# Two transformer layers on one core: fewer load-keeping matmuls, and a plan of the order made anew with other constants

## The chip, the cores and the metric

The kernel runs on one core of a Trainium2 chip. The metric is the device time in microseconds (us) of one execution. Engines: TensorE (PE in the profile; PEld is its weight load), VectorE (DVE), ScalarE (ACT), GpSimd (POOL), SyncE (SP), and the DMA queues.

## The reference

Attention and a feed-forward block, each twice, with the same weights in both rounds. x has 2048 rows of 448 numbers in bfloat16; 16 heads of 28; 1792 hidden features.

```python
def _A_ref(x, wqkv, wo):
    q, k, v = split_into_16_heads(x @ wqkv)
    p = softmax(q @ k.T * 28 ** -0.5)
    return heads_joined(p @ v) @ wo
def _B_ref(x, w1, b1, w2, b2):
    h = x @ w1 + b1
    r = where(h > 0, h, 0)
    return (r * r) @ w2 + b2
x = x + _A_ref(layernorm(x), ...)
x = x + _B_ref(layernorm(x), ...)
x = x + _A_ref(layernorm(x), ...)
x = x + _B_ref(layernorm(x), ...)
```

(Shortened: the splitting into heads and the einsums are written as products.)

## The kernel before

**Attention.** The 2048 queries stand in blocks of 256 (the last two of the second layer have 128), the 16 heads in four groups of four. A *unit* is one head, one block of queries and two tiles of 128 keys (four tiles, where the block has 128 queries): 512 score columns. A *score group* is three units: TensorE computes their scores with row-tiled matmuls of 32 rows (L969) into one of two score buffers in PSUM, three banks of 512 columns each. ScalarE turns them into probabilities with one exponential (L994, tile `pt<-sc`). For some groups ScalarE takes two units only (1024 columns for 1536), and the third is computed on VectorE and GpSimd by a polynomial: VectorE reads the scores (L1059), squares (L1076), GpSimd makes the power of two (L1083), VectorE multiplies (L1090). A score buffer is free for the group after the next once ScalarE, and where it has a part VectorE, have read it. The probabilities then go as the moving operand into column-tiled matmuls with V (L1153, `oT`), one *pass* for each block of queries and group of heads. Normalizing takes the sums out of `oT`: by transposes on VectorE (L1222 to L1238) near the end, elsewhere over DMAs (L1256 to L1280).

**The rest of a layer.** `chain` follows a finished block of queries: the product with wo, layernorm (L537 to L647), transposes on TensorE (L587, evicted at L599), the hidden layer with relu (L1347 on ScalarE, L1349 on VectorE) and square (L1354, L1356), the product with w2 (all of these full matmuls on L684), the sum with x (L1289), and for the first layer also the q, k and v of the second. These pieces are fitted in between the score groups; a score group stands on TensorE for each exponential.

**The order.** All of it is written out by a planner at build time. `Planner` keeps a clock for each engine, and generators (`s_stream` for scores, `e_stream` for exponentials, `p_stream` for passes, `chain`, `qkv` and others) offer operations with a duration, dependences and buffers. The planner takes the one that can start first, or by priority, advances the clock, and emits the instructions at once. So durations and latencies (`Op("PE", 0.227, ...)`, `LAT`, `PAIR`) cost nothing on the chip; they only set the order in each engine's queue. `PACE` changes constants of the planner from a given score group on, `FORCE` and `SKIP` name score groups whose third unit goes to VectorE, or doesn't, against the rule in `apart`. Queues on the chip run in the order written; waits on semaphores are put in by the framework.

**Unread matmuls.** Two kinds of matmuls only load TensorE. In `s_stream`, a score group's matmuls are issued again, once to three times (`MORE`), into the same banks with the same result, where the planner's load in a window of 3.4 us is under `HOT` and there is room. In `heat`, after a score group, one or two matmuls of 128x448 (L1407) go into a bank of the m pools that nobody reads, where the planned load over 2.8 us is under `HEAT`; their operands are `ident` and `xns[0]`, one of the buffers into which layernorm writes (`xn`):

```python
            short = HEAT - pl.load(WINDOW)
            if short <= 0 or not s_left or len(units) - at[0] < HSTOP:
                continue
            k = 1 if short < 0.14 else 2
...
                    nc.tensor.matmul(t[:, 0:D], lhsT=ident[:, :], rhs=xns[0][:, 0:D], start=True, stop=True)
```

At the start, before any input has landed, `warm_up` issues matmuls of zeros (L429).

Of the kernel before, what the change touches and what calls it, by code (L numbers as in the profile page):

```python
# [32 lines left out]
EPRIO = 2.5  # L33
ASIDE = 2.0
# [6 lines left out]
PRE = 0.5  # L41
# [8 lines left out]
L0N = 7.0  # L50
L1E = 1900
L1N = 5.6
MARGIN = 1.5
LOW = 0.85
# [11 lines left out]
SLACK = 0.5  # L66
WINDOW = 2.8
C_PRIO = 1.6
V_PRIO = 8.5
V_LATE = 4.6  # L70
V_LAST = 2.5
V_AGE = 6
V_PAST = 2
# [3 lines left out]
V_WAIT = 5  # L77
NEAR = 6
FAR = 9
KEEP = 6  # L80
LAG = 12
LEAD = 15
LAST = 690
BUSY = 0.97
TB = 2.2
TB2 = 0.9
SPAN = 15
# [2 lines left out]
AEND = 0  # L90
HOT = 0.9
MORE = 1
HEAT = 0.76
HWIN = 3.4
NEAR_U = 0
LASTP = 3.2
HOLD = 6
HOLD1 = 7
SOON = 0
# [6 lines left out]
CHUNK = 1  # L106
EV = 2.9
# [11 lines left out]
CUTS = (0, 10, 16)  # L119
CH = 4.0  # L120
QP = 8.0
FORCE = (26, 42, 46, 57, 59, 85, 86, 102, 105, 106, 107, 170, 171, 332, 335, 410, 413, 462, 466, 561, 563, 565, 567,
        576, 583, 584, 597, 598)
SKIP = (12, 13, 16, 18, 21, 22, 25, 29, 44, 47, 87, 151, 153, 154, 155, 168, 331, 333, 334, 372, 373, 375, 377, 412,
        559, 560, 562, 581, 595)
PACE = {
    0: {'ASIDE': 2.0, 'BUSY': 0.97, 'CH': 4.0, 'CHUNK': 1, 'C_PRIO': 1.6, 'EV': 2.9, 'FAR': 9, 'HOLD': 6,
         'KEEP': 6, 'L0N': 7.0, 'L1N': 5.6, 'LAG': 12, 'LASTP': 3.2, 'LEAD': 15, 'LOW': 0.85, 'MARGIN': 1.5,
         'MORE': 1, 'NEAR': 6, 'PRE': 0.5, 'QP': 8.0, 'SLACK': 0.5, 'SOON': 0, 'SPAN': 15, 'TB': 1.8, 'V_AGE':
         6, 'V_LAST': 1.8, 'V_LATE': 4.6, 'V_PRIO': 8.5, 'V_WAIT': 5},  # L130
    6: {'V_LATE': 3.5, 'C_PRIO': 2.6},
    12: {'HOLD': 4, 'KEEP': 2, 'V_LATE': 5.2},
    18: {'CHUNK': 3, 'V_LAST': 3},
    36: {'CHUNK': 2},
    54: {'QP': 5},
    60: {'V_AGE': 4},
    66: {'V_AGE': 5},
    84: {'BUSY': 0.995},
    90: {'NEAR': 8, 'BUSY': 0.97},
    96: {'NEAR': 6, 'BUSY': 0.995},  # L140
    114: {'NEAR': 8},
    150: {'LAG': 5, 'CH': 5, 'SOON': 0.5},
    156: {'MARGIN': 2.5, 'L0N': 6.0},
    162: {'TB': 2.2, 'KEEP': 5},
    174: {'KEEP': 2, 'HOLD': 5, 'LAG': 8},
    192: {'MORE': 2},
    198: {'MORE': 1, 'FAR': 12},
    204: {'NEAR': 6, 'EV': 1.5, 'PRE': -0.3},
    210: {'NEAR': 8, 'EV': 2.9, 'PRE': 0.5},
    216: {'KEEP': 3, 'V_WAIT': 3.5},  # L150
    240: {'LAG': 16, 'LASTP': 2.6, 'SPAN': 11},
    246: {'LAG': 8, 'LASTP': 3.2, 'SPAN': 15, 'MORE': 2, 'V_WAIT': 2.5},
    252: {'V_LATE': 4.0},
    282: {'MORE': 1},
    288: {'MORE': 2},
    306: {'CHUNK': 3},
    318: {'CHUNK': 2},
    360: {'ASIDE': 1.0, 'HOLD': 4},
    366: {'V_AGE': 3, 'L1N': 5.8},
    402: {'L1N': 5.0, 'CHUNK': 1, 'HOLD': 6},  # L160
    414: {'L1N': 5.8},
    426: {'HOLD': 5, 'SPAN': 20},
    432: {'LOW': 0.9},
    444: {'V_PRIO': 2.8},
    450: {'V_PRIO': 8.5},
    522: {'HOLD': 6, 'V_LATE': 4.6},
    528: {'HOLD': 5, 'V_LATE': 4.0},
    534: {'PRE': 0.8, 'L0N': 7.8, 'LOW': 0.95},
    540: {'ASIDE': 0.3, 'SPAN': 11},
    552: {'LAG': 5},  # L170
    576: {'FAR': 17},
    582: {'FAR': 12},
    588: {'FAR': 17, 'V_LAST': 3.5, 'SLACK': 0.2},
    594: {'V_LAST': 3, 'SLACK': 0.5},
    648: {'KEEP': 2, 'CHUNK': 2, 'LEAD': 12},
}


class Res:


    def __init__(self, n):
        self.n = n
        self.rel = []
# [4 lines left out]


class Op:
    __slots__ = ("eng", "dur", "fn", "deps", "acq", "rel", "mode", "sets", "start", "end", "res", "turn", "ready", "lat", "need", "got", "more", "room", "port", "durs")

    def __init__(self, eng, dur, fn, deps=(), acq=None, rel=None, mode="full", sets=(), lat=0.0, need=1, port=False):
        self.eng = eng if isinstance(eng, tuple) else (eng,)
        self.durs = dur if isinstance(dur, tuple) else (dur,) * len(self.eng)
        self.dur, self.fn, self.deps, self.mode, self.lat = self.durs[0], fn, deps, mode, lat
        self.rel = rel if isinstance(rel, list) else ([] if rel is None else [rel])
        self.acq = acq if isinstance(acq, tuple) or callable(acq) else (() if acq is None else (acq,))
        self.sets = sets if isinstance(sets, list) else ([sets] if sets else [])  # L200
        self.start = self.end = self.res = self.turn = None
        self.need, self.got, self.more, self.port = need, [], 0.0, port


LAT = {"PE": 0.25, "ACT": 0.28, "DVE": 0.07, "POOL": 0.10, "DMA": 2.0, "-": 0.0}
PAIR = {("PE", "ACT"): 0.275, ("PE", "DVE"): 0.197, ("DVE", "ACT"): 0.1, ("DVE", "POOL"): 0.1, ("DVE", "DVE"): 0.035,
        ("POOL", "DVE"): 0.035, ("PE", "PE"): 0.0, ("ACT", "ACT"): 0.0, ("POOL", "POOL"): 0.0}


class Planner:  # L210
# [20 lines left out]
        self.streams.sort(key=lambda s: s[0](0.0) if callable(s[0]) else s[0])  # L231

    def earliest(self, o):
        t = 0.0
        for d in o.deps:
            if not isinstance(d, Op):
                d = self.tok.get(d)
            if d is None or d.end is None:
                return None, None
            t = max(t, d.end + d.lat + PAIR.get((d.eng[0], o.eng[0]), LAT[d.eng[0]]))  # L240
        acq = o.acq() if callable(o.acq) else o.acq
        if o.acq:
            free = [r.when() for r in acq if r.when() is not None]
            if not free:
                return None, None
            t = max(t, min(free))
        o.ready = t
        best = None
        for e, dur in zip(o.eng, o.durs):
            s = max(t, self.clock[e])  # L250
            if e == "PE" and self.mode != o.mode:
                s = max(t, self.clock[e] + 0.1)
            if o.port:
                s = max(s, self.port["POOL"] - 0.14 if e == "DVE" else self.port["DVE"] + (0.01 if self.port["DVE"] > t else 0.0))
            late = s + (dur + ASIDE * (e == "DVE") if "POOL" in o.eng else 0.0)
            if best is None or late < best[2] - 0.05:
                best = (s, e, late)
        return best[:2]

    def run(self):  # L260
        while self.streams:
# [9 lines left out]
            if due is None:  # L271
                due = next((c[0] + c[3][2].dur + LAT["ACT"] for c in cands if c[1] == 1), None)
            if due is not None:
# [23 lines left out]
            for a in o.rel:  # L297
                a.got.append(o.end + o.lat + LAT[e])
                if len(a.got) == a.need:
# [9 lines left out]
def kernel(  # L309
# [44 lines left out]
    R_sc, R_m, R_pt = Res(2), (Res(1), Res(1)), Res(NPT)  # L354
# [24 lines left out]
    more = [const.tile([P, QR], DT.float32, name=f"more{g}") for a in AHEAD[3:] for g in a]  # L379
# [439 lines left out]
    for pi, (l, qb, g, kbs, first, last) in enumerate(passes):  # L819
        r = 4 // blocks[l][qb][1]  # L820
# [6 lines left out]
    gbuf = []  # L827
# [29 lines left out]
    def apart(i, now, us, soon=SOON):  # L857
# [20 lines left out]
        if any(pl.tok.get(d) is None or pl.tok[d].end + LAT["DVE"] > now for d in needs(units[j])):  # L878
            return None
        if len(gbuf) - 1 in FORCE:  # L880
            return j
        if len(gbuf) - 1 in SKIP or pl.load(SPAN, "DVE") > (LOW if behind(i) else BUSY):
            return None
# [19 lines left out]
    def s_stream():  # L903
        while at[0] < len(units):
            gi = len(gbuf)
# [5 lines left out]
            def fn(e, gi=gi, us=us, js=js):  # L911
# [50 lines left out]
                for i in list(range(4)) * (again + 1):  # L962
                    for k, (pi, kb, r, hh) in enumerate(us):
                        if i >= r:
# [5 lines left out]
                                         lhsT=K_sb[l][rows, g, (kb + i) * P:(kb + i + 1) * P],  # L970
                                         rhs=Q_sb[rows, g, t0 * P:(t0 + nt) * P],
                                         start=True, stop=True, tile_position=(DHP * hh, 0))
            o = gbuf[gi]["s"] = Op("PE", 0.227, fn,
                                   deps=list({d for u in us for d in needs(u)}), acq=R_sc, mode="row", sets=("s", gi))
            yield o
        s_left.clear()
# [8 lines left out]
    def e_stream():  # L985
        gi = 0
        while gi < len(gbuf) or s_left:
            yield Op("-", 0.0, None, deps=[("s", gi)])
            n = gbuf[gi]["n"] * 512

            def fn(e, gi=gi, n=n):
                e_now[:] = [e_now[0] + n // 512 + ("x" in gbuf[gi]), gi]
                pt = gbuf[gi]["pt"] = ptp.tile([P, 3 * 512], DT.bfloat16, name="pt")
                t = nc.scalar.activation(out=pt[:, 0:n], in_=gbuf[gi]["sc"][:, 0:n], func=AF.Exp,  # L994
                                         scale=float(np.log(2.0)) * 2.0 ** -FRAC)
                if gbuf[gi].get("x") is gbuf[gi]["s"]:
                    apart_from(gi, t)
            o = gbuf[gi]["e"] = Op("ACT", n / 1200 + 0.051, fn, deps=[("s", gi)], acq=R_pt, need=n // 512 + gbuf[gi].get("in", 0),
                                   rel=gbuf[gi]["s"], sets=("e", gi))
            yield o  # L1000
            gi += 1
# [390 lines left out]
    def heat():  # L1392


        for gi in itertools.count(HFROM):
            if not s_left:
                return
            yield Op("-", 0.0, None, deps=[("s", gi)])
            short = HEAT - pl.load(WINDOW)
            if short <= 0 or not s_left or len(units) - at[0] < HSTOP:  # L1400
# [57 lines left out]
```

## Time and profile before

| | us |
|---|---|
| median of 3 runs | 845.28 (845.02 to 845.38) |
| the profiled execution | 845.39 |
| its span, first to last instruction | 843.3 |
| first exponential starts (from the span's start) | 10.78 |
| last exponential ends | 828.78 |

| line, engine | what | count |
|---|---|---|
| L969 PE | score matmuls, repeats among them | 5120 |
| L1153 PE | probabilities with V | 4352 |
| L1407 PE | unread matmuls of `heat` | 133 |
| L994 ACT | exponentials, 1536 / 1024 columns | 445 / 238 |
| L1059 DVE | units taken from ScalarE | 237 |

In the lines of groups, a row gives line, engine, operation, tiles and shapes, count, then busy time in us, mean ns of one, and the engine's idle time before them with what ended it. In the timeline a row gives start in us, duration in us, engine, line, operation, tiles, shapes and count; idle time before it, and its releaser, stand in brackets. In the table by stretches a row gives the stretch, its length, busy us (and count) of PE, PEld, DVE, ACT and POOL, the granted clock of TensorE, the DMA share and GB/s.

### The profile page before, as it was taken

What the parts mean: (1) busy time and instruction counts of PE and PEld (TensorE: products, weight loads), DVE (VectorE), ACT (ScalarE), POOL (GpSimd) and SP (SyncE); (2) the same over time, 40 slices, a digit from 0 to 9 for tenths busy, and PEclk for the clock granted to TensorE, in tenths of its full rate; (3) what the DMA queues carried; (4) which work ended last, traced back from release to release, by engine and by line L of the source; (5) the groups of instructions that cost most, each with busy time, mean ns of one, the idle gap of its engine ahead of it and who ended that gap; (6) DMA issues with size and microseconds to landing.
All of it is one profiled execution on the core that took longest, in us unless ns stands there. A gap on an engine that the chain in (4) does not pass through costs nothing.

```text
span 843.3 us, 28075 instructions
## 1 busy us (share of the span) xinstructions
PE 805.7 (96%) x12089; PEld 422.3 (50%) x12089; DVE 788.5 (93%) x1531; ACT 827.2 (98%) x698; POOL 210.3 (25%) x332
## 2 busy tenths in 40 slices
PE   8999999999999999999999999999999999999997
PEld 4455544454544545455445444434455454545665
DVE  7999999999999999999999999999999998989954
ACT  8999999999999999999999999999999999999994
POOL 3211322322222223322222223322212223121200
PEclk9999999999999999999999999999999999999999
DMA  9200100000000000000000000011100001000000
GB/s 244 74 3 2 26 22 12 15 15 16 8 9 16 15 15 16 15 3 15 2 3 2 2 2 3 15 29 29 32 9 14 26 15 31 21 13 15 14 20 13
DMA packets 32312, 17.94 MB, mean 21 GB/s; under 512 B 17786, under 2 KB 31739, under 8 KB 32188
## 3 DMA queue, kind: packets, MB, share of 16 engines
q1 hardware_dynamic: 32188, 16.16, 7.0%
q8 instruction: 94, 1.54, 0.8%
q14 instruction: 30, 0.25, 0.1%
HBM read 13.87 MB, written 2.06 MB: 19 GB/s over the span
## 4 chain that ended last, share of the span: by engine, by line
ACT 43%; PE 33%; DVE 15%; issue 8%; POOL 1%; DMA 0%; ACTq 0%; DVEq 0%; POOLq 0%
ACT pt L994 43%; PE mt L684 13%; PE sc L969 11%; PE oT L1153 6%; DVE r L1349 2%; DVE v_i L1059 2%; DVE v_e L1076 1%; DVE pt L1090 1%; PE mt L1407 1%; PE sc L684 1%; PE tp L587 1%; DVE K_sb L1076 1%; DVE st L537 1%; DVE x_sb L1289 1%; DVE K_sb L1059 1%
## 5 line engine op out<-in xcount | busy, mean ns | idle before, releaser
L994 ACT ACTIVATE pt<-sc 128x1536 bf16<-128x1536 f32 (+1 forms) x683 | 816.9, 1464 | 1.7 <-PE sc L969 1.4
L969 PE MATMUL sc<-Q_sb,K_sb 32*128 32x256 bf16 (+1 forms) x5120 | 301.0, 265 | 27.7 <-ACT pt L994 20.7
L969 PEld LDWEIGHTS <-K_sb 32*128 32x128 bf16 x5120 | 128.6, 92 | 209.1 <-issue 160.7
L1083 POOL TENSOR_SCALAR v_i<-v_i 128x512 int32<-128x512 int16 x126 | 89.2, 708 | 291.8 <-DVE v_e L1076 290.2
L1153 PE MATMUL oT<-pt,V_sb 128*32 128x256 bf16 (+1 forms) x4098 | 157.0, 268 | 0.8 <-ACT pt L994 0.5
L684 PE MATMUL mt<-xnT,w 128*128 128x256 bf16 (+1 forms) x928 | 121.9, 269 | 0.6 <-DVE r L1349 0.3
L1153 PEld LDWEIGHTS <-V_sb 128*32 128x32 bf16 x4352 | 89.3, 96 | 52.9 <-issue 49.6
L684 PEld LDWEIGHTS <-w 128*128 128x128 bf16 x952 | 77.6, 98 | 36.4 <-issue 28.6
L1059 DVE TENSOR_SCALAR v_i<-sc 128x512 int32<-128x512 f32 x126 | 85.7, 682 | 5.2 <-PE sc L969 4.5
L1076 DVE SCALAR_TENSOR_TENSOR v_e<-v_i 128x512 f32<-128x512 uint16 x126 | 87.6, 699 | 0.3
L1083 POOL TENSOR_SCALAR K_sb<-K_sb 128x512 int32<-128x512 int16 x64 | 45.3, 708 | 138.6 <-DVE K_sb L1076 134.5
L1349 DVE TENSOR_SCALAR r<-mt 128x512 bf16<-128x512 f32 x108 | 73.7, 682 | 5.4 <-PE mt L684 4.7
L684 PE MATMUL mt<-w,V_sb 128*128 128x448 bf16 (+1 forms) x274 | 68.3, 352 | 0.0
L1083 POOL TENSOR_SCALAR V_sb<-V_sb 128x512 int32<-128x512 int16 x47 | 34.3, 729 | 101.6 <-DVE V_sb L1076 100.7
L1059 DVE TENSOR_SCALAR K_sb<-sc 128x512 int32<-128x512 f32 x64 | 43.7, 683 | 1.9 <-PE sc L969 1.6
L1289 DVE TENSOR_TENSOR x_sb<-x_sb,mt 128x448 bf16<-128x448 bf16 (+1 forms) x61 | 37.0, 607 | 8.9 <-PE mt L684 8.5
L1407 PE MATMUL mt<-xn,ident 128*128 128x448 bf16 x133 | 44.2, 355 | 1.1 <-DVE x_sb L1289 0.3
L1076 DVE SCALAR_TENSOR_TENSOR K_sb<-K_sb 128x512 f32<-128x512 uint16 x64 | 44.1, 694 | 0.1
L1090 DVE SCALAR_TENSOR_TENSOR pt<-v_e,v_i 128x512 bf16<-128x512 f32 x59 | 40.0, 679 | 3.8 <-POOL v_i L1083 3.8
L537 DVE BATCH_NORM_STATS2 st<-x_sb 128x6 f32<-128x448 bf16 x62 | 37.7, 611 | 0.8 <-DMA x_sb<-in_A_x_dram 0.6
L684 PEld LDWEIGHTS <-V_sb 128*128 128x128 bf16 x302 | 24.1, 98 | 25.1 <-issue 12.6
L1059 DVE TENSOR_SCALAR V_sb<-sc 128x512 int32<-128x512 f32 x47 | 31.9, 681 | 1.2 <-PE sc L969 1.0
(115 smaller groups left out, 828.0 us busy)
## 6 DMA issues: line engine op xcount, KB each, us to landing
rec<-scr SPq DMA_DIRECT2D x54, 128.0 KB
x_sb<-in_A_x_dram SPq DMA_DIRECT2D x8, 224.0 KB
out_dram<-x_sb SPq DMA_DIRECT2D x15, 112.0 KB
w<-in_B_w_dram SPq DMA_DIRECT2D x1, 1568.0 KB
w<-in_B_w_dram SPq DMA_DIRECT2D x1, 1344.0 KB
dn<-oT_sb SPq DMA_DIRECT2D x54, 4.0 KB
V_sb<-in_A_wqkv_dram SPq DMA_DIRECT2D x4, 168.0 KB
scr<-dn SPq DMA_DIRECT2D x27, 8.0 KB
```

What stands on the lines that cost most here:

```text
L537: nc.vector.bn_stats(out=box["st"][:, :], in_=x_sb[:, t0 + j, :] if src is None else src())
L684: nc.tensor.matmul(box["t"][:, c0:c0 + n], lhsT=lhsT() if callable(lhsT) else lhsT, rhs=rhs, start=a, stop=b)
L969: nc.tensor.matmul(dst[k][:, i * nt * P:(i + 1) * nt * P], lhsT=K_sb[l][rows, g, (kb + i) * P:(kb + i + 1) * P], rhs=Q_sb[rows, g, t0 * P: ...
L994: t = nc.scalar.activation(out=pt[:, 0:n], in_=gbuf[gi]["sc"][:, 0:n], func=AF.Exp, scale=float(np.log(2.0)) * 2.0 ** -FRAC)
L1059: t = nc.vector.tensor_scalar(out=box["i"], in0=two(src), scalar1=EXP_BIAS, scalar2=EXP_LOW, op0=ALU.add, op1=ALU.max)
L1076: nc.vector.scalar_tensor_tensor(out=box["h"], in0=box["f"], scalar=lin, in1=box["f"], op0=ALU.add, op1=ALU.mult)
L1083: (nc.vector if e == "DVE" else nc.gpsimd).tensor_scalar(out=box["e"], in0=box["n"], scalar1=2.0 ** 22, scalar2=EXP_BASE, op0=ALU.mult, op ...
L1090: nc.vector.scalar_tensor_tensor(out=box["two"](pd), in0=box["h"], scalar=low, in1=box["e"].bitcast(DT.float32), op0=ALU.add, op1=ALU.mult)
L1153: nc.tensor.matmul(box["t"][DHP * hh:DHP * hh + DHP, 0:n], lhsT=V_sb[l][:, kb + i, 4 * g + hh, :], rhs=p[:, c0:c0 + n], start=begin and kb ...
L1289: nc.vector.tensor_tensor(out=x_sb[:, tb, lo:hi], in0=x_sb[:, tb, lo:hi], in1=t[:, 0:hi - lo], op=ALU.add)
L1349: nc.vector.tensor_scalar(out=r[:, 0:w], in0=t[:, 0:w], scalar1=0.0, scalar2=None, op0=ALU.max)
L1407: nc.tensor.matmul(t[:, 0:D], lhsT=ident[:, :], rhs=xns[0][:, 0:D], start=True, stop=True)
```

## The change

`HEAT` goes from 0.76 to 0.5. `FORCE`, `SKIP` and `PACE` are replaced by other lists (`PACE` now steps by 8 score groups, and sets `EPRIO` and `V_PAST` too, and no longer `LAG`, `NEAR`, `FAR`, `ASIDE`, `QP`, `V_LATE`, `V_PRIO` and `V_WAIT`). Some of the planner's durations and latencies get other values. `earliest` keeps the time at which an operation's dependences are met in a new field `known`, and doesn't work it out again. The engine code (which operations, tiles and buffers there are) is the same.

```diff
-HEAT = 0.76
+HEAT = 0.5
...
-FORCE = (26, 42, 46, 57, 59, 85, 86, 102, 105, 106, 107, 170, 171, 332, 335, 410, 413, 462, 466, 561, 563, 565, 567,
-        576, 583, 584, 597, 598)
...
+FORCE = (63, 65, 67, 69, 70, 72, 74, 76, 77, 78, 128, 132, 134, 144, 148, 149, 151, 162, 181, 190, 200, 201, 205, 207,
+        244, 245, 392, 396, 409, 413, 456, 548, 550, 641, 644, 645, 647)
...
 PACE = {
...
-    6: {'V_LATE': 3.5, 'C_PRIO': 2.6},
-    12: {'HOLD': 4, 'KEEP': 2, 'V_LATE': 5.2},
...
+    24: {'EPRIO': 8, 'L0N': 7.4},
+    40: {'HOLD': 5},
...
-LAT = {"PE": 0.25, "ACT": 0.28, "DVE": 0.07, "POOL": 0.10, "DMA": 2.0, "-": 0.0}
-PAIR = {("PE", "ACT"): 0.275, ("PE", "DVE"): 0.197, ("DVE", "ACT"): 0.1, ("DVE", "POOL"): 0.1, ("DVE", "DVE"): 0.035,
+LAT = {"PE": 0.25, "ACT": 0.3, "DVE": 0.07, "POOL": 0.10, "DMA": 2.0, "-": 0.0}
+PAIR = {("PE", "ACT"): 0.275, ("PE", "DVE"): 0.2, ("DVE", "ACT"): 0.1, ("DVE", "POOL"): 0.15, ("DVE", "DVE"): 0.035,
...
     def earliest(self, o):
-        t = 0.0
-        for d in o.deps:
...
+        t = o.known
+        if t is None:
+            t = 0.0
+            for d in o.deps:
...
+            o.known = t
...
-            o = gbuf[gi]["s"] = Op("PE", 0.227, fn,
+            o = gbuf[gi]["s"] = Op("PE", 0.234, fn,
...
-            o = gbuf[gi]["e"] = Op("ACT", n / 1200 + 0.051, fn, deps=[("s", gi)], acq=R_pt, need=n // 512 + gbuf[gi].get("in", 0),
+            o = gbuf[gi]["e"] = Op("ACT", n / 1200 + 0.0555, fn, deps=[("s", gi)], acq=R_pt, need=n // 512 + gbuf[gi].get("in", 0),
```

More of the change, by code (lines that the diff above doesn't have):

```diff
@@ L121 @@
 QP = 8.0
-FORCE = (26, 42, 46, 57, 59, 85, 86, 102, 105, 106, 107, 170, 171, 332, 335, 410, 413, 462, 466, 561, 563, 565, 567,
-        576, 583, 584, 597, 598)
-SKIP = (12, 13, 16, 18, 21, 22, 25, 29, 44, 47, 87, 151, 153, 154, 155, 168, 331, 333, 334, 372, 373, 375, 377, 412,
-        559, 560, 562, 581, 595)
-PACE = {
[L127 to L130, printed above, removed]
-    6: {'V_LATE': 3.5, 'C_PRIO': 2.6},
-    12: {'HOLD': 4, 'KEEP': 2, 'V_LATE': 5.2},
[L133 to L175, printed above, removed]
@@ new lines @@
+FORCE = (63, 65, 67, 69, 70, 72, 74, 76, 77, 78, 128, 132, 134, 144, 148, 149, 151, 162, 181, 190, 200, 201, 205, 207,
+        244, 245, 392, 396, 409, 413, 456, 548, 550, 641, 644, 645, 647)
+SKIP = (66, 73, 80, 81, 83, 84, 87, 135, 150, 164, 165, 178, 180, 183, 184, 188, 243, 246, 247, 281, 283, 285, 286,
+        312, 313, 317, 318, 319, 379, 381, 382, 408, 410, 412, 415, 544, 545, 549, 551, 553, 554, 643, 653, 654, 656,
+        657, 658, 659, 661)
+PACE = {
+    0: {'BUSY': 0.97, 'CH': 4.0, 'CHUNK': 2, 'C_PRIO': 1.6, 'EPRIO': 2.5, 'EV': 2.9, 'HOLD': 6, 'KEEP': 6,
+         'L0N': 7.0, 'L1N': 5.6, 'LASTP': 3.2, 'LEAD': 15, 'LOW': 0.85, 'MARGIN': 1.5, 'MORE': 1, 'PRE': 0.5,
+         'SLACK': 0.5, 'SOON': 0, 'SPAN': 15, 'TB': 2.2, 'V_AGE': 6, 'V_LAST': 2.5, 'V_PAST': 2},
+    24: {'EPRIO': 8, 'L0N': 7.4},
+    40: {'HOLD': 5},
+    48: {'SOON': 1.0, 'MARGIN': 4.5},
+    56: {'TB': 1.8, 'LOW': 0.9},
+    72: {'SPAN': 8, 'L1N': 5.0, 'TB': 3.6},
+    80: {'SPAN': 15, 'L1N': 5.6, 'TB': 1.8},
+    112: {'V_LAST': 3.5},
+    128: {'MARGIN': -1},
+    160: {'MARGIN': 4.5},
+    168: {'MARGIN': -1, 'CH': 5, 'PRE': 0.8, 'HOLD': 3},
+    176: {'LEAD': 12},
+    184: {'LEAD': 15},
+    200: {'V_AGE': 5, 'L1N': 5.8, 'V_LAST': 1.8},
+    208: {'V_AGE': 6, 'L1N': 5.6, 'V_LAST': 3.5},
+    216: {'BUSY': 1.01},
+    232: {'KEEP': 3},
+    240: {'EPRIO': 1.5},
+    256: {'MORE': 3, 'HOLD': 5},
+    272: {'TB': 2.2},
+    280: {'EPRIO': 8, 'LASTP': 2.6},
+    312: {'V_PAST': 5, 'EV': 2.2},
+    344: {'EV': 3.3},
+    352: {'MARGIN': 0.5},
+    384: {'C_PRIO': 3.2},
+    392: {'MARGIN': 4.5, 'CHUNK': 1},
+    400: {'L0N': 7.8, 'KEEP': 4},
+    408: {'CH': 3.3},
+    456: {'KEEP': 2},
+    640: {'HOLD': 3},
+    648: {'HOLD': 5},
+    656: {'SLACK': 0.2},
@@ L191 @@
 class Op:
-    __slots__ = ("eng", "dur", "fn", "deps", "acq", "rel", "mode", "sets", "start", "end", "res", "turn", "ready", "lat", "need", "got", "more", "room", "port", "durs")
+    __slots__ = ("eng", "dur", "fn", "deps", "acq", "rel", "mode", "sets", "start", "end", "res", "turn", "ready", "lat", "need", "got", "more", "room", "port", "durs", "known")
     def __init__(self, eng, dur, fn, deps=(), acq=None, rel=None, mode="full", sets=(), lat=0.0, need=1, port=False):
@@ L200, in __init__ @@
         self.sets = sets if isinstance(sets, list) else ([sets] if sets else [])
-        self.start = self.end = self.res = self.turn = None
+        self.start = self.end = self.res = self.turn = self.known = None
         self.need, self.got, self.more, self.port = need, [], 0.0, port
-LAT = {"PE": 0.25, "ACT": 0.28, "DVE": 0.07, "POOL": 0.10, "DMA": 2.0, "-": 0.0}
-PAIR = {("PE", "ACT"): 0.275, ("PE", "DVE"): 0.197, ("DVE", "ACT"): 0.1, ("DVE", "POOL"): 0.1, ("DVE", "DVE"): 0.035,
+LAT = {"PE": 0.25, "ACT": 0.3, "DVE": 0.07, "POOL": 0.10, "DMA": 2.0, "-": 0.0}
+PAIR = {("PE", "ACT"): 0.275, ("PE", "DVE"): 0.2, ("DVE", "ACT"): 0.1, ("DVE", "POOL"): 0.15, ("DVE", "DVE"): 0.035,
         ("POOL", "DVE"): 0.035, ("PE", "PE"): 0.0, ("ACT", "ACT"): 0.0, ("POOL", "POOL"): 0.0}
@@ L233, in earliest @@
     def earliest(self, o):
-        t = 0.0
-        for d in o.deps:
[L236 to L240, printed above, removed]
+        t = o.known
+        if t is None:
+            t = 0.0
+            for d in o.deps:
+                if not isinstance(d, Op):
+                    d = self.tok.get(d)
+                if d is None or d.end is None:
+                    return None, None
+                t = max(t, d.end + d.lat + PAIR.get((d.eng[0], o.eng[0]), LAT[d.eng[0]]))
+            o.known = t
         acq = o.acq() if callable(o.acq) else o.acq
         if o.acq:
-            free = [r.when() for r in acq if r.when() is not None]
+            free = [w for w in (r.when() for r in acq) if w is not None]
             if not free:
```

## The prediction

> **What bounds the kernel now.** I read the busy shares first, then ScalarE's groups by form, then the starts of single exponentials, and last the places where one starts late.
>
> ```profile
> span 843.3 us, 28075 instructions
> PE 805.7 (96%) x12089; PEld 422.3 (50%) x12089; DVE 788.5 (93%) x1531; ACT 827.2 (98%) x698; POOL 210.3 (25%) x332
> PEclk9999999999999999999999999999999999999999
> ```
> Three engines look full; the shares alone don't decide. ScalarE's groups, by form:
>
> ```profile
> L994 ACT ACTIVATE pt<-sc 128x1536 bf16<-128x1536 f32 x445 | 649.5, 1611 | 1.7 <-PE sc L969 1.4
> L994 ACT ACTIVATE pt<-sc 128x1024 bf16<-128x1024 f32 x238 | 270.2, 1190 | 0.0
> ```
> The durations overlap (445 x 1611 ns is more than 649.5 us), so what counts is the distance from start to start. Neighbours without a wait, and the last one:
>
> ```profile
> 26.45 1.47 ACT L994 ACTIVATE pt<-sc 128x1536 bf16<-128x1536 f32 x1
> 27.78 1.49 ACT L994 ACTIVATE pt<-sc 128x1536 bf16<-128x1536 f32 x1
> ...
> 30.44 1.08 ACT L994 ACTIVATE pt<-sc 128x1024 bf16<-128x1024 f32 x1
> 31.35 1.10 ACT L994 ACTIVATE pt<-sc 128x1024 bf16<-128x1024 f32 x1
> ...
> 827.45 1.34 ACT L994 ACTIVATE pt<-sc 128x1024 bf16<-128x1024 f32 x1
> ```
> A large one takes 1.330 us, a small one 0.903 (unrounded starts). The first starts at 10.78, the last ends at 828.78: a stream of 818.00 us. Its work is 445 x 1.330 + 237 x 0.903 + 1.34 = 807.2 us. So the span is 10.8 (opening) + 807.2 (exponentials) + 10.8 (late starts) + 14.5 (after the last). ScalarE sets the end, and only the three small terms, or fewer exponentials, can give anything.
>
> I went through the starts of all 683. Of the 10.8 us, 7.6 are in 54 exponentials over 40 ns late; the rest is jitter. By what stands on TensorE just ahead of the late score matmuls: 1.4 us in the opening (three, before 45 us), 2.2 in 16 behind an unread matmul of L1407, 0.8 in five whose scores are computed twice or more, 3.2 in 30 behind useful matmuls. One of the 16:
>
> ```profile
> 441.66 0.38 PE L684 MATMUL mt<-xnT,wq 128*128 128x256 bf16 x2
> 442.24 0.35 PE L1407 MATMUL mt<-xn,ident 128*128 128x448 bf16 x1 [0.19 <-DVE xn L647]
> 442.52 0.39 PE L969 MATMUL sc<-Q_sb,K_sb 32*128 32x256 bf16 x6
> ```
> The unread matmul reads xn, which VectorE was just writing; in TensorE's queue the score waits behind it, starts 0.28 us after it, and its exponential (443.02) is 0.23 us late.
>
> **The change, part by part.** It alters the planner's constants and lists, so I took the order of instructions from both built programs and priced it by rows of before.
>
> Exponentials: 444 large and 239 small in place of 445 and 238: 0.903 - 1.330 = -0.43 us on the path. The part goes to VectorE instead: 238 chains in place of 237, three VectorE operations that stand 0.60 apart, +1.8 us. VectorE is busy 775 of the stream's 818 us; that idle time covers it; without the cover it costs 1.8.
>
> Unread matmuls of L1407: 133 become 4. At 0.189 us each (four of 128x448 on L684 start 0.189 apart) TensorE gets 24.4 us back. Repeated scores, also unread, go the other way: L969 has 5300 matmuls for 5120, 30 more repeats of six. A repeat costs 0.21 us (12 take 0.61, 6 take 0.40): +6.4 us. Switches between row-tiled, column-tiled and full matmuls fall from 1404 to 1324; a switch adds 0.095 us (0.285 from a 448-column matmul to a score, 0.189 to its like): -7.6. Together -25.6 us of TensorE's issue time, some 769 before. None of it is on the path by itself: the stream of exponentials covers it. What reaches the path is lateness:
> - Behind L1407: 2.2 us, of which 0.30 (at 136.97) was held by VectorE's read of the old scores and stays. The others are late by at most 0.23, less than the 0.28 that an unread matmul puts ahead of the score. I take -1.9 (bounds -2.2 and 0, if another wait stands right behind).
> - Repeats: 170 sets make 0.8 us late; 30 more, at the same rate, +0.14 (bounds 0 and 30 x 0.21 = 6.3, if all came too late; nearest the measured rate).
> - The 3.2 us behind useful matmuls: the emptier queue should take some of it, a new order deals new ones. I take -0.9; bounds -3.2 (all gone) and +3.2 (twice as many).
> - Opening: the order is the same up to the 12 scores at 22.01. In after, four more matmuls of wq (4 x 0.109) stand ahead of them, waiting for a bank that K's eviction at 21.27 frees: +0.45 (bounds 0 and 0.5).
> - End: 14 full matmuls stand between the last wo matmul and the four transposes, in place of 13: +0.2 (bounds 0 and 0.5; below nothing is out, the chain behind is the same).
>
> The planner's durations (score 0.234 for 0.227, exponential +0.0045, three waits) emit nothing; they act through the order counted here. SP's queue has the same 184 issues, POOL one more power operation of 0.71 us at 25% load.
>
> Sum: -0.43 - 1.9 - 0.9 + 0.14 + 0.45 + 0.2 = -2.4 us. The profiled execution took 845.39 (2.1 around its span); the median shown is 845.28, 0.1 less. 845.39 - 2.4 - 0.1 = 842.9; I say 842.8.
>
> [...] L1407 keeps TensorE loaded, and the floor falls from 0.76 to 0.5. Counting only the time in which the array gets columns, the least loaded 3.4 us before the last exponentials end have 0.47, at full clock:
>
> ```profile
> 824.50:827.90 3.40, 2.36 (x67) 1.77 (x56) 1.50 (x5) 3.40 (x4) 0.00 (x0) 1.00 0.02 5
> ```
> (2.36 is PE busy, with ends that overlap; 1.00 the granted clock.) By the order of after, three score groups in a row (about 3.6 us) fall to 0.30 of ScalarE's time near group 454, and to 0.36, 0.39 and 0.42 at three other places; before, never under 0.46. So after goes where this trace shows nothing. [...]
>
> **The rivals.**
> - *VectorE holds the scores (slower).* Place: a score must wait until VectorE has read the third part of the scores two groups back (L1059); an exponential late by 0.30 us at 136.97 is that. It decides once VectorE is some 0.9 us behind. For it: VectorE has 95% of ScalarE's time filled, and the stretches between two such reads that hold more VectorE work than exponentials rise from 91 to 100. Against: summed along the order, the backlog over 0.9 us falls from 0.8 us to 0.4. If 20 of the 100 paid 0.30: 842.8 + 6 = 848.8.
> - *The clock drops (slower).* For it: the loads above. Against: 0.47 did nothing. The first matmuls, from 1.25 on, stand 0.37 apart for 0.189, and full speed is there by 7.7: some 6.5 us at half clock. 74% (median load) of that, 4.8 us, less 0.8 of spare time (12%) and 0.7 that the queue may lag, is 3.3 a place: 846.1 with one, 849.4 with two, 856 with four.
> - *The relief is hidden (same).* The scores behind L1407 were waiting for VectorE or a bank anyhow; L1407 filled the wait. For it: it is issued only where the planner saw room. Then -1.9 and -0.9 fall out: -0.43 + 0.14 + 0.45 + 0.2 = +0.4, 845.6.
> - *It doesn't do what it says.* TensorE has 51 more matmuls in all; but cheaper ones, by the count above. That changes no time of its own.
>
> **How the numbers follow.** 0.2% is 1.7 us, about what a measurement of this kernel tells from no change: faster is below 843.6, slower above 847.0. Forecast 0.54 (839 to 843.6), hidden relief 0.18 (843.6 to 847), VectorE 0.20 (847 to 850), clock 0.08 (846 to 856, mostly slower). So faster 0.54, same 0.18, slower 0.28. The likeliest one's own range is 839 to 843.6. If all lateness behind L1407 and behind useful matmuls went, with no repeat, opening or end cost, it is 845.3 - 0.4 - 2.2 - 3.2 = 839.5, and some jitter may go with it: low 838.6. High 848.8, the price of VectorE's case; beyond it lie the upper parts of two rivals, together with what is below the low some 0.17.
>
> **What would show it.** Right: L994 x444 and x239, the stream near 815.8 us with late starts of 8.8 us in place of 10.8; L1407 x4; few late scores behind L1407; first stall at 22 us up from 0.88 to some 1.3; clock 1.00 throughout; end near 14.7. Wrong: late starts of 11 us or more, the late scores ended by DVE L1059 (VectorE), or a clock row below 9 near 430 or 560 us (clock). An end over 15.5, or an opening that loses more than 1 us, would break the sum where I took it as nearly fixed.

## The result, and the profile after

The changed kernel takes 847.85 us (median of 11 runs, 845.23 to 849.88), the kernel before 845.32 (11 runs, 845.02 to 846.76): a ratio of 1.0023, 95% interval 1.0015 to 1.0032. It is slower, by 0.23%, where 842.8 was forecast. Its lines are numbered 11 lower than those of before (L983 is the old L994, L958 the old L969, L1396 the old L1407). The page's first lines and the clock row, in tenths, one digit for each fortieth of the span:

```profile
span 845.7 us, 28161 instructions
PE 787.9 (93%) x12140; PEld 424.3 (50%) x12140; DVE 787.5 (93%) x1533; ACT 827.8 (98%) x699; POOL 215.0 (25%) x333
...
PEclk9999999999999999999999999899999999999999
```

TensorE is less busy, ScalarE is as before, and one digit of the clock is an 8, at 529 to 550 us. ScalarE's exponentials by form:

```profile
L983 ACT ACTIVATE pt<-sc 128x1536 bf16<-128x1536 f32 x444 | 652.7, 1631 | 2.8 <-PE sc L958 2.6
L983 ACT ACTIVATE pt<-sc 128x1024 bf16<-128x1024 f32 x239 | 275.7, 1202 | 1.4 <-PE sc L958 1.4
```

The counts are those of the built program; idle time before them is 4.2 us for 1.7. By stretches of 3.41 us (PE, PEld, DVE, ACT and POOL busy, then the granted clock):

```profile
537.61:541.03 3.42, 2.39 (x50) 1.29 (x52) 3.42 (x8) 3.42 (x4) 0.84 (x2) 1.00 0.00 0
541.03:544.44 3.41, 3.39 (x47) 1.95 (x46) 2.38 (x5) 3.17 (x3) 1.42 (x2) 0.50 0.06 7
544.44:547.85 3.41, 3.41 (x57) 1.69 (x51) 1.97 (x4) 2.39 (x3) 0.62 (x1) 0.50 0.26 79
547.85:551.27 3.42, 2.65 (x54) 1.56 (x47) 2.98 (x7) 3.42 (x4) 1.54 (x2) 1.00 0.04 5
551.27:554.68 3.41, 2.52 (x62) 1.68 (x62) 3.29 (x7) 3.41 (x4) 0.62 (x1) 1.00 0.07 13
554.68:558.09 3.41, 2.40 (x47) 1.53 (x44) 3.34 (x6) 3.41 (x4) 0.62 (x1) 1.00 0.23 68
558.09:561.51 3.42, 3.42 (x47) 0.99 (x39) 2.76 (x6) 2.71 (x3) 0.62 (x1) 0.50 0.02 5
```

The clock is at one half from 541.03 to 547.85 and from 558.09 to 561.51. Scores then take twice as long (repeated sets of six matmuls start 0.43 us apart at 546 us, and 0.22 at full clock), and ScalarE waits, as its timeline shows (idle time in brackets):

```profile
540.57 1.65 ACT L983 ACTIVATE pt<-sc 128x1536 bf16<-128x1536 f32 x1
542.38 4.09 ACT L983 ACTIVATE pt<-sc 128x1024 bf16<-128x1024 f32 x3 [0.16 <-PE sc L958]
547.40 1.02 ACT L983 ACTIVATE pt<-sc 128x1024 bf16<-128x1024 f32 x1 [0.93 <-PE sc L958]
```

The exponentials in and just behind the two stretches are late by 3.3 us in sum. Worked out from the starts of all 683, as in the prediction, the span moved so:

| term, us | before | after | difference |
|---|---|---|---|
| first exponential starts | 10.78 | 10.48 | -0.29 |
| one exponential less of 1.330, one more of 0.903 | | | -0.43 |
| late starts, 0 to 45 us | 1.47 | 1.26 | -0.21 |
| late starts, 45 to 520 us | 5.90 | 6.20 | +0.30 |
| late starts, 520 to 590 us | 0.82 | 3.90 | +3.08 |
| late starts, from 590 us | 2.62 | 2.33 | -0.29 |
| last exponential's start to the end | 15.86 | 16.07 | +0.21 |
| span | 843.3 | 845.7 | +2.4 |

All the loss is in the stretch with the half clock. The runs say the same: at a mean clock of 1.000 the changed kernel took 845.23 (one run), at 0.998 846.36 to 846.58 (four), at 0.996 848.08, at 0.994 847.85 to 849.44 (four), at 0.992 849.88. One window of 3.41 us at half clock lowers the mean by 0.002, so a window costs about 1.2 us. And even the undisturbed run gains nothing on before: two things have to be explained.

### The profile page after: what moved, and what is told of

The parts are those of the page before. It is cut to its first block, busy times and chain, and to the rows that moved or that the text cites. A ratio compares the mean times of both kernels' runs of the same rounds, so it can differ in the third digit from the quotient of the medians.

```text
span 845.7 us, 28161 instructions
## 1 busy us (share of the span) xinstructions
PE 787.9 (93%) x12140; PEld 424.3 (50%) x12140; DVE 787.5 (93%) x1533; ACT 827.8 (98%) x699; POOL 215.0 (25%) x333
## 4 chain that ended last, share of the span: by engine, by line
ACT 46%; PE 29%; DVE 15%; issue 8%; DMA 0%; POOL 0%; SPq 0%; ACTq 0%; DVEq 0%; POOLq 0%
ACT pt L983 46%; PE mt L673 12%; PE sc L958 11%; PE oT L1142 5%; DVE v_i L1048 2%; DVE v_e L1065 1%; DVE pt L1079 1%; DVE r L1338 1%; PE sc L673 1%; DVE x_sb L1278 1%; DVE K_sb L1048 1%; DVE K_sb L1065 1%; DVE st L526 1%; DVE V_sb L1048 1%; DVE V_sb L1065 1%
## 5 line engine op out<-in xcount | busy, mean ns | idle before, releaser
L983 ACT ACTIVATE pt<-sc 128x1536 bf16<-128x1536 f32 (+1 forms) x683 | 817.0, 1481 | 4.2 <-PE sc L958 4.0
L958 PE MATMUL sc<-Q_sb,K_sb 32*128 32x256 bf16 (+1 forms) x5300 | 311.4, 267 | 47.6 <-ACT pt L983 41.5
L958 PEld LDWEIGHTS <-K_sb 32*128 32x128 bf16 x5300 | 140.8, 92 | 220.6 <-issue 172.6
L673 PE MATMUL mt<-xnT,w 128*128 128x256 bf16 (+1 forms) x912 | 119.7, 270 | 1.0 <-DVE oT_sb L1168 0.5
L1072 POOL TENSOR_SCALAR K_sb<-K_sb 128x512 int32<-128x512 int16 x66 | 47.2, 715 | 146.9 <-DVE K_sb L1065 145.7
L1338 DVE TENSOR_SCALAR r<-mt 128x512 bf16<-128x512 f32 (+1 forms) x109 | 74.0, 680 | 4.4 <-PE mt L673 3.9
L673 PE MATMUL mt<-w,V_sb 128*128 128x448 bf16 x274 | 68.5, 355 | 0.0
L1072 POOL TENSOR_SCALAR V_sb<-V_sb 128x512 int32<-128x512 int16 x45 | 32.6, 724 | 103.2 <-DVE V_sb L1065 99.7
L1278 DVE TENSOR_TENSOR x_sb<-x_sb,mt 128x448 bf16<-128x448 bf16 x61 | 37.3, 611 | 9.1 <-PE mt L673 8.8
L553 POOL TENSOR_TENSOR ve<-mv,eps_t 128x2 f32<-128x2 f32 (+1 forms) x34 | 12.5, 368 | 106.4 <-DVE mv L531 105.8
L673 PEld LDWEIGHTS <-V_sb 128*128 128x128 bf16 x302 | 24.9, 97 | 25.4 <-issue 11.4
L1079 DVE SCALAR_TENSOR_TENSOR pt<-v_e,v_i 128x512 bf16<-128x512 f32 x51 | 35.0, 692 | 1.9 <-POOL v_i L1072 1.8
```

The source lines that it names most:

```text
L553: nc.gpsimd.tensor_tensor(out=ve[:, a:b], in0=mv[0][:, a:b, 1], in1=eps_t[:, a:b], op=ALU.add)
L673: nc.tensor.matmul(box["t"][:, c0:c0 + n], lhsT=lhsT() if callable(lhsT) else lhsT, rhs=rhs, start=a, stop=b)
L958: nc.tensor.matmul(dst[k][:, i * nt * P:(i + 1) * nt * P], lhsT=K_sb[l][rows, g, (kb + i) * P:(kb + i + 1) * P], rhs=Q_sb[rows, g, t0 * P: ...
L1072: (nc.vector if e == "DVE" else nc.gpsimd).tensor_scalar(out=box["e"], in0=box["n"], scalar1=2.0 ** 22, scalar2=EXP_BASE, op0=ALU.mult, op ...
L1079: nc.vector.scalar_tensor_tensor(out=box["two"](pd), in0=box["h"], scalar=low, in1=box["e"].bitcast(DT.float32), op0=ALU.add, op1=ALU.mult)
L1278: nc.vector.tensor_tensor(out=x_sb[:, tb, lo:hi], in0=x_sb[:, tb, lo:hi], in1=t[:, 0:hi - lo], op=ALU.add)
```

## The experiments

The theories: A, the clock halves after a window of some 3.4 us with little work in the array, weighted by the rows and columns that a matmul uses; B, it follows TensorE's busy time; C, chance. For the missing gain: the unread matmuls of L1407 caused the lateness behind them (as predicted), or they only filled a wait.

**e1, a full matmul in 40 score groups.** In the loop of `s_stream`, ahead of the scores, into the score bank:

```diff
+                if 432 <= gi < 472:
+                    nc.tensor.matmul(dst[0][:, 0:D], lhsT=ident[:, :], rhs=w2[:, 0, 0:D], start=True, stop=True)
                 for i in list(range(4)) * (again + 1):
```

> The changed kernel with one unread matmul of 128x448, full array, ahead of the scores of each of the score groups 432 to 471 (about 530 to 580 us); the order of all else is the same. Theory A (the clock halves when the work in the array, weighted by the rows and columns that a matmul uses, is low over a window of some 3.4 us: 0.38 and 0.32 in the two windows before the drops at 541 and 558 us, never under 0.40 elsewhere): the pad adds some 0.14, so the clock stays at 1.00 there in every run, and the median falls from 847.9 to 845 to 846. Theory B (the clock follows the time in which TensorE is busy, whatever the shape): the same here, so this run alone does not tell A from B; its twin with a narrow matmul does. Theory C (the drop is chance, or comes from elsewhere): drops stay, the median stays near 847.9.

850.87 us (850.65 to 851.21, 4 runs), ratio 1.0063 [1.0047, 1.008]. No half clock between 500 and 600 us in the profile; the runs are at 0.998 to 1.000. The drop is gone in this trace, and of the ten runs of e1 and e2 none is under 0.998, where six of eleven of the changed kernel are; so C falls. But the median went up and not down: 40 pads put ahead of the scores make late starts of their own (15.0 us in sum, none at half clock). The miss is in what a pad costs.

**e2, the same on 32 rows.**

```diff
+                if 432 <= gi < 472:
+                    nc.tensor.matmul(dst[0][:, 0:D], lhsT=ident[DHP * us[0][3]:DHP * us[0][3] + DHP, :],
+                                     rhs=w2[DHP * us[0][3]:DHP * us[0][3] + DHP, 0, 0:D], start=True, stop=True,
+                                     tile_position=(DHP * us[0][3], 0))
```

> As e1, but the unread matmul uses 32 of the 128 rows, with the same 448 columns and about the same time. Theory A: it adds only a quarter of the work, some 0.04, so the windows before 541 and 558 us stay near 0.36 to 0.42 and the clock still drops in most runs; median 846.5 to 849. Theory B: as good as the full one, clock 1.00 and 845 to 846.

847.70 us (847.33 to 849.34, 6 runs), 1.0029 [1.0018, 1.0041]; five runs at 1.000, one at 0.998. Theory A expected drops, and there were none. In the profiled run the weighted load of the padded windows came to 0.42 at the least, above where anything dropped elsewhere (0.38 at the most), so the pair does not tell A from B.

**e3, before without L1407.** Planned as before, the time in the plan kept, no matmul issued:

```diff
             def junk(e):
-                t = bank(o, "mt")
-                for _ in range(k):
-                    nc.tensor.matmul(t[:, 0:D], lhsT=ident[:, :], rhs=xns[0][:, 0:D], start=True, stop=True)
+                pass
```

> The kernel before, planned as it was, but without the 133 unread matmuls of L1407; all else in the same order. Prediction's reason (late exponentials behind L1407 vanish): outside of stretches at half clock the late starts fall by about 1.9 us, from 10.8 to some 8.9. Rival (they waited for something else): late starts stay at 10.5 or more. Theory A: without them the weighted load falls to 0.18 to 0.30 in windows near 544 to 568 us, so the clock drops there and the median is 2 us or more above before, 847 to 853. Theory B: plain busy time falls less; few drops, 843 to 846.

848.69 us (847.23 to 850.09, 5 runs), 1.0039 [1.0025, 1.0052], clock 0.984 to 0.990. In the profiled run it halves at 546.4, 556.7 and 566.9 us. Outside of 520 to 590 us the late starts are 1.47 + 5.78 + 2.49 = 9.74 us; before had 1.47 + 5.90 + 2.62 = 9.99. So taking L1407 away gave 0.25 us there. Exponential by exponential: the 16 that the prediction puts behind L1407 were late by 2.21 us in sum, and are late by 1.39 without it. That sum hides two kinds. Eleven of the 16 now come on time (0.07 us left of 1.13), the prediction's own example among them: its score no longer waits for xn, and the exponential that was 0.23 late at 443.02 is on time, the next one (0.26 in before) too:

```profile
441.91 0.27 PE L684 MATMUL mt<-xnT,wq 128*128 128x256 bf16 x1
442.12 0.39 PE L969 MATMUL sc<-Q_sb,K_sb 32*128 32x256 bf16 x6
```

The other five are late without L1407 as well (1.08 us with it, 1.32 without). And exponentials elsewhere became later: outside of 520 to 590 us all gains add up to 1.97 us, all losses to 1.72. One place shows how. In before, a score at 158.17 stands behind L1407 at 157.88, and its exponential is 0.13 late. In e3 the unread matmul is gone, but a bias row, L684, waits for VectorE's eviction, and the score comes at 158.35:

```profile
156.95 0.40 PE L969 MATMUL sc<-Q_sb,K_sb 32*128 32x256 bf16 x6
157.50 0.35 PE L684 MATMUL mt<-b2w,one 128*128 128x448 bf16 x1 [0.16 <-DVE oT_sb L1179]
157.69 0.73 PE L684 MATMUL mt<-w,K_sb 128*128 128x448 bf16 x3
158.35 0.39 PE L969 MATMUL sc<-Q_sb,K_sb 32*128 32x256 bf16 x6
```

The exponential is now 0.38 late. VectorE is behind here since GpSimd's rstd came later, first in before, then in e3:

```profile
153.18 0.70 DVE L647 TENSOR_SCALAR xn<-x_sb,mv,rstd 128x448 bf16<-128x448 bf16 x2 [0.58 <-POOL rstd L565]
153.56 0.70 DVE L647 TENSOR_SCALAR xn<-x_sb,mv,rstd 128x448 bf16<-128x448 bf16 x2 [0.85 <-POOL rstd L565]
```

With the filler gone, another wait decided. The other losses were not followed up like this.

**e4, before with L1407 on 32 rows.** Count, order, bank and columns as before:

```diff
-                    nc.tensor.matmul(t[:, 0:D], lhsT=ident[:, :], rhs=xns[0][:, 0:D], start=True, stop=True)
+                    nc.tensor.matmul(t[:, 0:D], lhsT=ident[0:DHP, :], rhs=xns[0][0:DHP, 0:D], start=True, stop=True,
+                                     tile_position=(0, 0))
```

> The kernel before with its 133 unread matmuls on 32 of the 128 rows: the same count, order, bank, operand tile and about the same time. Theory A: as good as none for the clock, drops near 545 to 568 us, 847 us or more. Theory B: clock 1.00, 845 to 846.

850.77 us (849.77 to 854.33, 4 runs), 1.007 [1.0047, 1.0093], all at 0.986 to 0.990. The stretches of e4 around its drop:

```profile
557.88:561.29 3.41, 3.08 (x40) 1.37 (x42) 3.41 (x8) 3.41 (x4) 0.62 (x1) 1.00 0.04 2
561.29:564.71 3.42, 2.84 (x44) 1.21 (x44) 3.38 (x9) 3.42 (x4) 0.62 (x1) 1.00 0.28 84
564.71:585.19 20.48, 20.25 (x184) 8.15 (x179) 16.14 (x29) 16.38 (x14) 5.05 (x7) 0.50 0.08 20
```

and of before at the same place:

```profile
560.00:563.40 3.40, 2.90 (x43) 1.07 (x36) 3.40 (x8) 3.40 (x5) 0.62 (x1) 1.00 0.16 47
563.40:566.80 3.40, 3.15 (x41) 1.25 (x44) 3.37 (x8) 3.40 (x4) 1.60 (x3) 1.00 0.14 38
```

TensorE is busy 2.84 of 3.42 us, as in before, and the clock halves for 20.5 us; the changed kernel kept it behind 2.52 of 3.41 (551.27). Busy time doesn't decide. Theory B falls; what differs in e4 is how many rows the filler uses (and with that its tile of the array).

**e5, eight pads.** As e1, for `gi in (442, 445, 449, 451, 455, 456, 462, 466)`.

> The changed kernel with one unread full matmul of 128x448 ahead of the scores of only eight score groups (442, 445, 449, 451, 455, 456, 462, 466), those with over 0.65 us of free TensorE time; all else in the same order. Theory A (the clock halves after a window of some 3.4 us in which the work weighted by rows and columns is under some 0.35 to 0.38): the two low windows rise by some 0.06 to 0.11 each, to 0.42 to 0.45; no drop between 500 and 600 us, 1.00 in the middle. Then this run tells what the new order is worth by itself: 842.8 to 843.6 if the prediction's relief is there and only the clock hid it; 845.0 to 845.8 if the new order has as many late starts as the old one (10.4 us in the changed kernel's profile outside of the drops). If drops are not tied to the load: median 847 to 848 as the changed kernel.

845.94 us (845.54 to 847.54, 11 runs), 1.0008 [0.9999, 1.0016]. Eight runs at 1.000 took 845.54 to 846.14; three at 0.998, 847.30 to 847.54. With the clock held, the new order is no faster than the old one: the late starts are 11.4 us, for 10.8 in before (1.3 of them belong to what e6 takes out).

**e6, e5 without repeats where two units share rows.** In a score group whose three units include two of the same head of the group of four, their matmuls use the same 32 rows. In the changed kernel's timeline:

```profile
482.58 0.40 PE L958 MATMUL sc<-Q_sb,K_sb 32*128 32x256 bf16 x6
482.91 0.55 PE L673 MATMUL mt<-wv,xnT 128*128 128x448 bf16 x2
483.50 1.47 PE L958 MATMUL sc<-Q_sb,K_sb 32*128 32x256 bf16 x18
```

18 matmuls take 1.47 us, where others of 18 take 0.83 (at 539.59): those start in threes, six times 0.109 us apart; these start by ones and twos, twelve times 0.109 apart.

```diff
-                for i in list(range(4)) * (again + 1):
+                for i in list(range(4)) * (again + 1 if len({u[3] for u in us}) == len(us) else 1):
```

> As e5, and the scores are not repeated in the three groups (of 683) in which two of the three units have the same 32 rows of the array; repeats elsewhere stay, the order stays. In the changed kernel's profile a set of six takes 0.44 us in such a group and not 0.21, and three exponentials behind them are late by 0.55, 0.52 and 0.25. If the repeats there are the cause: 0.8 to 1.3 us below e5. If something else holds these exponentials: within 0.3 of e5.

845.00 us (844.54 to 849.53, 12 runs), 1.0 [0.9989, 1.0011]; eight runs at 1.000, 844.54 to 846.17. That is 0.9 us under e5, by all runs and by those at 1.000. The same place in e6:

```profile
483.06 0.40 PE L960 MATMUL sc<-Q_sb,K_sb 32*128 32x256 bf16 x6
483.39 0.55 PE L673 MATMUL mt<-wv,xnT 128*128 128x448 bf16 x2
483.98 0.59 PE L960 MATMUL sc<-Q_sb,K_sb 32*128 32x256 bf16 x6
```

The exponential behind it, late by 0.55 in e5, is on time, the one at 576 us (0.44 in e5) as well. The third group in which matmuls went away stands at 555 us, and its exponential (0.35 in e5) is on time too. The 0.25 of the expectation is another exponential's, at 653 us, whose scores are not repeated; it is late by 0.25 in both. Against these 1.3 us, an exponential at 104 us is late by 0.37 in e6 and by 0.02 in e5; nothing that e6 changes touches it, and it is late in the profiles of e1, e2 and e10 too, and not in that of the changed kernel.

**e7, the same in before.**

> The kernel before without repeats in its three groups that have two units on the same rows; the order stays. Late there by 0.14, 0.12 and about 0.2 us. If the repeats are the cause: 0.3 to 0.5 us below before, 844.7 to 845.0; otherwise 845.2.

844.86 us (844.70 to 846.42, 11 runs), 0.9993 [0.9984, 1.0001]. At 1.000 its ten runs took 844.70 to 845.00, and 23 of before on the same chip 844.93 to 845.32. The three groups that lost matmuls stand at 74, 103 and 545 us, and all three exponentials behind them (0.14, 0.12 and 0.21 late in before) came on time.

**e8, before planned anew.** The planner knows that such groups take longer, and doesn't repeat them:

```diff
-                o.more = 0.22 * again
+                again *= len({u[3] for u in us}) == len(us)
+                o.more = 0.22 * (again + (len({u[3] for u in us}) < len(us)))
```

> The kernel before, planned again with one thing more known to the planner: scores of two units on the same rows take 0.22 us more, and are not repeated. The order differs from the third part of the opening on, with the lists of choices unchanged. A new order that nobody searched for: if late starts are mostly a matter of the order dealt, anything from 844 to 852, with late starts behind useful matmuls other than the 2.5 to 3.2 us of before; if the order matters little, 844.7 to 845.2.

869.41 us (868.48 to 871.13, 4 runs), 1.028 [1.0266, 1.0295]. One wait makes 15.2 of the 24 us, and the end behind the last exponential's start is 8.6 us longer:

```profile
499.53 26.48 ACT L995 ACTIVATE pt<-sc 128x1536 bf16<-128x1536 f32 x22
541.18 1.94 ACT L995 ACTIVATE pt<-sc 128x1024 bf16<-128x1024 f32 x2 [15.17 <-PE sc L970]
```

Scores of the second layer had to wait for its last keys, behind the last products of a feed-forward block, a layernorm and a projection. The same lists of choices with one thing more known to the planner are another order, and a worse one than I had allowed for.

**e9 and e10, the least that holds the clock.** e9 is e7 with L1407 kept only in the score groups 425 to 479; e10 is e6 with pads in 442, 445, 455 and 456 only.

```diff
+                if 425 <= len(gbuf) < 480:
...
-                if gi in (442, 445, 449, 451, 455, 456, 462, 466):
+                if gi in (442, 445, 455, 456):
```

> As e7 (the kernel before without repeats in groups with two units on the same rows), and L1407's unread matmuls issued only in the score groups 425 to 479: 43 of 133 stay, where e3's clock dropped; the order stays. In e3, outside of 520 to 590 us, the late starts fell by 0.25 us only (11.8 less 9.99 would be the prediction's 1.9). If so here: full clock, 0.1 to 0.3 us below e7, 844.6 to 844.8 at full clock. If L1407 was the cause of lateness, as predicted: 843.3 to 843.8. If the other 90 were needed for the clock: drops, above 846.

(The bracket in it is a slip: the late starts outside of 520 to 590 us are 9.99 and 9.74.) e9: 846.16 us (844.58 to 850.26, 12 runs), 1.0009 [0.9996, 1.0022]; five runs at 1.000 took 844.58 to 845.35, not the 843.3 to 843.8 of the prediction's reason. The other seven had drops. In the profiled run one is in the opening, at 7.33, which the kernel before, by its times, has in some runs too (see the end), and one at 123.4 us, where two of L1407's matmuls were now missing. Four runs are at 0.996 or less, where none of the 23 of before beside them is under 0.998: the other 90 were needed for the clock too.

> As e6, with four of the eight unread full matmuls (groups 442, 445, 455, 456). Each pad in e5 seems to cost at most 0.05 us. If drops need the weighted load of a whole window under some 0.38: mostly full clock, 844.4 to 845.0, with drops in a few more runs than e6 (1 of 12). If the eight were all needed: drops in most runs, 846 and more.

e10: 846.03 us (844.33 to 849.63, 11 runs), 1.0009 [0.9995, 1.0022]; three runs at 1.000 took 844.33 to 844.70, eight had drops, five of them at 0.996 or less, for one of e6's twelve (on another chip). Four pads are too few. No version beats the kernel before by more than its interval; e7 comes nearest.

## Why the prediction was wrong

**The clock.** "The clock drops" was one of the rivals, with a chance of 0.08; it is what happened, in ten of eleven runs. Its lowest place was right: the 0.30 near group 454 lies in the window ahead of the drop at 558.09 (that group's exponential starts at 555.02). Ahead of 541.03 stand groups 441 to 444; whether they are one of its three other places isn't on record. The step that failed is the one that took the array's time with columns as the load ("0.47 did nothing"), and so left the clock out of the sum. That measure counts a column of any matmul alike. Weighted by rows x columns / 128 x 128, over windows of 3.41 us laid along the clock's changes, from about 45 us on, drops followed 0.38 and 0.32 (after), 0.34, 0.31 and 0.18 (e3), 0.33 (e4) and 0.32 (e9), and 0.06 in e8's long wait; the lowest that kept the clock are 0.36 (e9, e10) and 0.37 (e3, e4), and before has 0.40 or more wherever a window is laid. Without the weights the two mix: drops behind 0.25 to 0.56 (e8's apart), none behind 0.44 and 0.45. L1407's matmuls stand in the trace with 128 x 128 rows and columns, a score with 32 x 128 and a product with V with 128 x 32, a quarter of that; scores start three at once (at 539.59 in after within 0.01 us, the next three 0.11 later), products with V four (at 305.33 in before, the same times); that 129 full ones went and 180 narrow ones came was in the prediction's count, and only their time was looked at. e4 shows the rows' part (with the tile that goes with them); no run varied the columns. One window that dropped, 0.38 (after), lies among those that kept it, so the limit is not sharper than that by this measure.

That the clock would hold at loads under those of before, and the sum so need no term for it, no trace showed. In the window before the drop at 541.03 TensorE was busy 2.39 of 3.42 us, its longest wait was 0.51, and the clock halved. The rival's price was too high: 3.3 us a place, where the place at 541.03 cost 1.9 and the one at 558.09 1.1. The first was as long as assumed (6.83 us for 6.5), the second half of that; and the price used the median load, 74%, where the windows ahead of these drops have 0.50 and 0.56 by the same measure.

**Behind L1407, -1.9 us.** Wrong as a sum: 0.25 us came out of the whole of it in e3's undisturbed stretches. The cause was read rightly at most of the places, since eleven of the 16 exponentials came on time without L1407. Of the five that didn't, one (136.97) was forecast to stay, one (546.26) was held by the repeats that e7 takes out, and one (521.80) has transposes and not L1407 ahead of it in the trace. The step that failed is to take the sum of the single places as the gain: other exponentials got later by nearly as much. That is the bound of 0 that the term named ("if another wait stands right behind"). "The relief is hidden" was the right rival by its size; its reason, that these scores were waiting anyhow, fits five of the 16 at most.

**Behind useful matmuls, -0.9 us.** Not there. Outside of the half clock the late starts of the new order are what the old one had: +0.30 from 45 to 520 us, -0.29 from 590 on. Without the repeats on shared rows the two orders come out alike: late starts of 10.7 us in e6 and 10.5 in e7, and a median of 844.8 for both at full clock. TensorE's time that was freed (busy 787.9 us for 805.7) went into idle time on TensorE, which is not the bound. Whether the new constants or the lists made the order no better wasn't taken apart; e8 shows only how much an order can matter.

**Repeats, +0.14 us.** Mis-sized: the price of 0.21 us a set holds for three different rows; on shared rows a set takes 0.44 (from 483.50 in after). In the three groups with shared rows repeats made 0.55, 0.44 and 0.35 us late (e5), and e6 got 0.9 us back; in before the like made 0.14, 0.12 and 0.21 late, and e7 got 0.2 us back at full clock.

**The rest.** Exponentials, -0.43: as built. End, +0.2: 0.21, of which 0.19 stands between the last wo matmul and the transposes, where it was put. Opening, +0.45: the stall at 22 us did grow, by 0.19 to 1.06, but one at 41 us went, -0.21 in all. The first exponential's start, -0.29, was not in the sum; it differs by nearly as much from profile to profile (10.62 in e4, 10.88 in e3, with the same instructions ahead).

## What to carry to other kernels

A filler on an idle engine can have a second job: before taking it away, ask what it keeps up (here the clock: 0.998 to 1.000 with L1407, 0.984 to 0.990 without it, e3), and measure that in its own unit, not in busy time (e4). A late instruction behind a filler may be late because of it, and the whole still gain little when the filler goes (eleven of 16 came on time in e3, for 0.25 us in sum), where the next wait decides; the same plan with the filler left out tells, exponential by exponential and in sum. And time freed on an engine that doesn't set the end can be worth nothing until the waits that do are named: here 17.8 us of TensorE's went, and the late starts outside of the half clock came to 9.79 us for 9.99.

## What the runs showed of the hardware

- The clock is at 1.0 or 0.5, for whole multiples of 3.41 us: 6.83 and 3.41 in after, 10.24 in e3, 20.48 in e4. Where the windows lie differs from profile to profile (the first at full clock starts at 7.07 us in before, 5.13 in after, 4.64 in e1). By the mean clock the changed kernel had one to four half windows from run to run, or none; that the windows' place is the reason isn't shown.
- The opening can lose one too. In e1, e2 and e9 the clock halves at 8.06, 7.81 and 7.33 us, and the first exponential starts at 12.39, 12.27 and 12.21 and not at 10.5 to 10.9. Six of 29 runs of the kernel before beside e5 are at 0.998 and take 846.6 to 846.8, 1.6 us more than the others.
- The windows ahead of these three have a weighted load of 0.36, 0.34 and 0.32, about as the other windows that dropped; the opening windows of e10 and e4 with 0.38 and 0.43 kept the clock. Whether the transposes on TensorE (L576, in before L587) belong in that load, these traces don't decide: without them the three have 0.23, 0.21 and 0.20, and e10's 0.26; but counted so, windows of e4 with 0.30 and of e3 with 0.33 kept the clock later on, while 0.34 and 0.38 dropped.
